# A second-stage table with zeros cleared on the chip and weight columns 128 apart, an inverse on 64-row tiles, and a new order of the operations

## The chip, the core and the metric

The kernel runs on one core of a Trainium2 chip. The metric is the device time of one execution in microseconds. The core has five engines that run side by side and meet at semaphores: TensorE (PE in the profile, its weight loads PEld), VectorE (DVE), ScalarE (ACT), GpSimd (POOL) and SyncE (SP), which here issues nearly all DMAs.

## The reference, cut to what matters

Two kinds of layers alternate, each twice, on a sequence of 2048 rows of 512 channels in bf16: a convolution layer A and a two-layer perceptron B.

```python
def _A_ref(q, k, v, shift_k, ssm_k, ssm_D):
    for t in range(ks):                       # ks = 4
        k_shift = k_shift + k_pad[:, t:t + S, :] * shift_k[:, ks - 1 - t][None, None, :]
    kv = k_shift * v
    kv_f = rfft(kv padded to 2 * S along the sequence)
    kf_f = rfft(ssm_k padded to 2 * S)
    y = irfft(kv_f * kf_f)[first S rows]
    y = y + kv * ssm_D[None, None, :]
    return q * y

def _B_ref(x, w1, b1, w2, b2):
    y = _layernorm(x, axis=-1)
    h = _gelu(jnp.einsum("bsd,df->bsf", y, w1) + b1)
    return jnp.einsum("bsf,fd->bsd", h, w2) + b2

x = A_q
x = x + _A_ref(_layernorm(x), A_k, A_v, A_shift_k, A_ssm_k, A_ssm_D)
x = x + _B_ref(_layernorm(x), B_w1, B_b1, B_w2, B_b2)
x = x + _A_ref(_layernorm(x), A_k, A_v, A_shift_k, A_ssm_k, A_ssm_D)
x = x + _B_ref(_layernorm(x), B_w1, B_b1, B_w2, B_b2)
```

The convolution of `k_shift * v` with `ssm_k` doesn't depend on `x`, so the kernel computes it once and uses it in both A layers. `ssm_D` is folded into the filter's first tap.

## The kernel before, in words

**The convolution as matmuls.** The sequence is treated as two halves of 1024 rows. Each half goes through a transform of two stages on TensorE. The first stage (`stage1`, matmuls on line 553) works on 64 groups of 8 channels and writes a real and an imaginary part to the two column halves of the array, 16 matmuls to a tile (a tile here is a piece of the accumulator memory, PSUM, that one group of matmuls fills and one or two evictions empty). The second stage (`stage2`, line 565) has 128 weight matrices of 128 x 128, one for each frequency index, in an on-chip table `R_S2` of 128 partitions x 16384 elements; a tile is 16 matmuls, each with its own weight load and 64 streamed columns. Eight tiles make one transform. It is used four times: the filter's first and second half (operations tagged `h2_0` and `h2_1`) and the signal's (`x2_0` and `x2_1`). Each weight matrix is mostly zeros: the 8 channels of a group don't mix, so an input partition (real or imaginary, position a, channel d) feeds only the 16 outputs of the same channel d. The table comes from memory with its zeros, 4 MB, in 16 DMAs (`tload` with `t_s2`). After it stand products on DVE (line 464 through `tt`), half of them with a copy of the filter whose real and imaginary partitions are exchanged by DMA (`swap`).

The inverse has two stages as well. `inverse1` (line 665) multiplies with two small tables in `R_U` (128 x 128 each), 16 matmuls of 128 streamed columns to a tile, in pairs that accumulate, and 8 tiles to a half (`i1_0`, `i1_1`). Its weights are the products, read with a distance of 4 elements between columns. `inverse2` (line 683) follows (`i2_0`, `i2_1`). `turn` (line 536) and `shift_turn` (line 585) transpose on TensorE; the weights of `turn` are read 8 elements apart, those of `shift_turn` and `stage2` contiguously. The short shift filter is `shift` (line 610, matmuls of 64 rows in two row halves of the array) and `shift_pair` (line 638, four row quarters).

**The rows.** The rows of half 0 go through both pairs of layers in blocks of 128 or 256 rows, those of half 1 in blocks of 512: statistics (tags `q`, `z`; DVE and POOL), normalising (lines 822 and 823), products and sums (`y`), a transpose, the first matrix (`m1`, line 886) with the gelu on ACT (line 891), the second matrix (`m2`, line 920) with the sum on DVE (line 924). Half 0 can start when the inverse of the first half is done; the second half's transforms run between the `m1` and `m2` matmuls of half 0.

**The order.** The builder first lists 1185 operations, each with the engines that can run it, a duration and what it reads and writes. Three hand-made tables then settle everything: `SEQ` (the order of all operations), `ENGS` (the engine of those that have a choice) and `BANKS` (the PSUM banks of each tile). Each engine gets its operations in the order of `SEQ` and runs them strictly in that order; `sync` puts in the semaphore waits. Operations 4 to 15 load the filter's, k's and v's first half; 16 to 31 are the 16 table loads. In the order before, the table loads stand on SP between the loads of the first 25 us. The eviction helper is `evac` (ACT on line 469, DVE on line 470).

Of the kernel before, what the change touches and what calls it, by code (L numbers as in the profile page):

```python
# [36 lines left out]
class Prog:  # L37
# [4 lines left out]
    G = 4  # L42
    LAT = 155.0
    SEQ = (
# [53 lines left out]
    ENGS = ("apvpvvvpavaavaaaaaavvvaaavvvpvpvaavaaaaavaavvaaaaaaaavavaaaaaavaaavaaaaaappppaaaaaaaaaaaaaaaaaaaaaaaaaaaaapvvp"  # L98
            "paappvppaappvvvpaappaappaappaappaappaappvavpaappvappaappvvppvvvpaappvvavvvvvvavpvvvvppavavpvvvvvpvaaavpvvaaapv"
            "avva")  # L100
    BANKS = ("02220326464004602026041320002442462264542202240064064646402046462667062260046446220462640604660406064226644472"
             "44450442172316353547502206314500451400554567076567013226140174645320543403764701436154766316307007062272260403"
# [243 lines left out]
def _tables():  # L346
# [9 lines left out]
    c, s = np.cos(th), np.sin(th)  # L356
# [604 lines left out]
```

## Time and profile before

| what | value |
|---|---|
| median of 3 runs | 238.67 us (238.3 to 239.51) |
| profiled execution, its span | 238.6 us |
| ScalarE, VectorE busy | 67%, 75% of the span |
| moved by DMA | 26.75 MB |
| mean granted TensorE clock | 0.993 |

The span is that of one execution under the profiler. A row of a group gives the line, the engine, the operation, the names and shapes, how often it occurs, the busy time, the mean of one in ns, and the idle time of its engine before it with what ended it. Matmuls are pipelined: the duration of one is longer than the distance to the next, so what a matmul costs in a stream is read from the start of a run of them to the start of what follows, as the chain of waits gives it. In a table by stretches each engine's busy time in us stands with its number of instructions, and the last columns are the granted clock, the DMA engines' share and the GB/s moved.

### The profile page before, as it was taken

The page shows a single profiled execution, that of the slowest core. Times are in us where ns is not written, and L with a number is a line of the kernel's source. Part 1 is how long each engine was busy: PE and PEld are TensorE (multiplying, and loading weights), DVE is VectorE, ACT ScalarE, POOL GpSimd, SP SyncE. Part 2 cuts the span into 40 slices and gives each one's busy share as a digit, 9 for nine tenths or more (in the row PEclk, how much of TensorE's full clock was granted, in tenths as well). Part 3 has the DMA queues.
Part 4 walks back from the last instruction along what each step waited for, and adds up shares of the span by engine and source line. Part 5 has one row for each costly group of instructions (what it writes and reads, how often), then busy time and mean ns, then how long its engine had stood idle before and what let it go on. Part 6 is the DMA issues. An engine that isn't in the chain of part 4 may idle for free.

```text
span 238.6 us, 6251 instructions
## 1 busy us (share of the span) xinstructions
PE 226.9 (95%) x2615; PEld 152.3 (64%) x2637; DVE 178.1 (75%) x358; ACT 159.6 (67%) x255; POOL 55.3 (23%) x120
## 2 busy tenths in 40 slices
PE   6998698899999999999999999999999999999995
PEld 3897588885968588667769675644445444444454
DVE  0579869999999999999999999593579469404013
ACT  2586879999996899999768786359036606831630
POOL 2421030104623506446004522303020210200000
PEclk9999979999999999999999999999999999999999
DMA  6999767989946660053100304200300050132202
GB/s 173 350 393 388 272 181 186 257 267 194 163 87 197 153 140 3 1 69 103 54 0 15 80 0 83 49 3 12 78 0 3 18 157 0 25 66 91 84 0 91
DMA packets 41112, 26.75 MB, mean 112 GB/s; under 512 B 23702, under 2 KB 33788, under 8 KB 41084
## 3 DMA queue, kind: packets, MB, share of 16 engines
q1 hardware_dynamic: 40786, 26.20, 40.5%
q8 instruction: 21, 0.34, 0.6%
q10 hardware_dynamic: 298, 0.16, 0.3%
q14 instruction: 7, 0.06, 0.1%
HBM read 15.07 MB, written 2.10 MB: 72 GB/s over the span
## 4 chain that ended last, share of the span: by engine, by line
PE 83%; DVE 6%; DMA 4%; ACT 3%; issue 2%; POOL 1%; SPq 1%; POOLq 0%
PE ps L886 32%; PE ps L920 31%; PE ps L665 6%; PE ps L553 5%; PE ps L565 3%; ACT ar L469 3%; DMA ar<-in_A_ssm_k_dram 2%; DVE ar L464 2%; DMA ar<-ar 2%; DVE ar L616 1%; PE ps L683 1%; PE ps L909 1%; PE ps L638 1%; PE ps L610 1%; DVE ar L470 1%
## 5 line engine op out<-in xcount | busy, mean ns | idle before, releaser
L891 ACT ACTIVATE ar<-ps,sm 128x256 bf16<-128x256 f32 (+4 forms) x143 | 65.4, 525 | 41.0 <-PE ps L886 39.5
L469 ACT ACTIVATE ar<-ps 128x1024 bf16<-128x1024 f32 (+3 forms) x77 | 71.3, 1005 | 16.4 <-PE ps L553 6.4
L886 PE MATMUL ps<-ar 128*128 128x256 bf16 (+4 forms) x568 | 81.5, 297 | 0.3
L920 PE MATMUL ps<-ar 128*128 128x512 bf16 (+1 forms) x324 | 77.2, 379 | 1.1 <-issue 0.3
L886 PEld LDWEIGHTS ps<-ar 128*128 128x128 bf16 (+1 forms) x572 | 52.8, 100 | 28.1 <-ACT ar L891 0.4
L464 DVE TENSOR_TENSOR ar<-ar 128x512 bf16<-128x512 bf16 (+3 forms) x105 | 62.7, 637 | 0.9 <-ACT ar L469 0.4
L920 PEld LDWEIGHTS ps<-ar 128*128 128x128 bf16 (+1 forms) x341 | 32.4, 98 | 33.4 <-ACT ar L891 0.2
L924 DVE TENSOR_TENSOR ar<-ar,ps 128x512 bf16<-128x512 bf16 x31 | 20.7, 678 | 33.2 <-PE ps L920 33.0
L797 DVE BATCH_NORM_STATS2 sm<-ar 128x6 f32<-128x512 bf16 x64 | 42.9, 683 | 0.5
L822 ACT ACTIVATE ar<-ar,sm 128x512 bf16<-128x512 bf16 x34 | 26.4, 811 | 9.5 <-DVE sm L809 8.3
L804 POOL TENSOR_TENSOR sm<-sm 128x2 f32<-128x2 f32 (+2 forms) x26 | 23.6, 909 | 23.8 <-DVE sm L802 22.0
L802 POOL TENSOR_SCALAR sm<-sm 128x2 f32<-128x2 f32 (+2 forms) x21 | 6.4, 304 | 97.3 <-DVE sm L798 97.1
L553 PE MATMUL ps<-ar 128*64 128x128 bf16 x512 | 18.6, 227 | 3.1 <-issue 1.4
L565 PEld LDWEIGHTS ps<-ar 128*128 128x128 bf16 x512 | 18.4, 102 | 3.4 <-ACT ar L469 1.0
L565 PE MATMUL ps<-ar 128*128 128x64 bf16 x512 | 19.6, 199 | 0.5 <-ACT ar L469 0.4
L553 PEld LDWEIGHTS ps<-ar 128*64 128x64 bf16 x512 | 15.7, 114 | 6.1 <-issue 2.6
L812 POOL TENSOR_SCALAR sm<-sm 128x1 f32<-128x1 f32 x43 | 16.1, 390 | 2.0
L470 DVE CAST ar<-ps 128x1024 bf16<-128x1024 f32 x11 | 13.3, 1222 | 4.3 <-PE ps L565 2.8
L665 PE MATMUL ps<-ar 128*128 128x128 bf16 x256 | 15.0, 219 | 0.5 <-DVE ar L464 0.4
L665 PEld LDWEIGHTS ps<-ar 128*128 128x128 bf16 x256 | 14.7, 113 | 1.2 <-DVE ar L464 0.6
L823 DVE TENSOR_SCALAR ar<-ar,sm 128x512 bf16<-128x512 bf16 x30 | 11.8, 410 | 3.4 <-POOL sm L812 3.1
L470 DVE COPY ar<-ps 128x1024 bf16<-128x1024 bf16 (+1 forms) x9 | 5.5, 632 | 8.0 <-PE ps L516 5.3
(41 smaller groups left out, 94.3 us busy)
## 6 DMA issues: line engine op xcount, KB each, us to landing
ar<-tab_s SPq DMA_DIRECT2D x16, 256.0 KB, 9.0
ar<-ar SPq DMA_DIRECT2D x16, 256.0 KB, 3.7
ar<-in_A_ssm_k_dram SPq DMA_DIRECT2D x8, 256.0 KB, 6.8
ar<-in_A_q_dram SPq DMA_DIRECT2D x8, 256.0 KB, 4.7
ar<-in_A_v_dram SPq DMA_DIRECT2D x8, 256.0 KB, 6.1
out_dram<-ar SPq DMA_DIRECT2D x7, 256.0 KB, 2.5
ar<-in_B_w_dram SPq DMA_DIRECT2D x4, 344.0 KB, 4.8
ar<-in_B_w_dram SPq DMA_DIRECT2D x5, 256.0 KB, 4.0
```

The source lines that it names most:

```text
L464: return P.op(eng, lambda e: e.tensor_tensor(o, a, b, op), dur, reads=[a, b] + list(more), writes=[o])
L469: return e.activation(dst, src(), AF.Copy)
L470: return e.tensor_copy(dst, src())
L553: r = e.matmul(Q(tl, 64 * ri, 64, i * 128, [1, 128]), w, m, start=True, stop=True)
L565: r = e.matmul(Q(tl, 0, 128, i // 8 * 512 + i % 8 * 4, [32, 16], [1, 4]), w, m, start=True, stop=True)
L665: r = e.matmul(Q(tl, 0, 128, i * 128, [1, 128]), w, m, start=n == 0, stop=n == 1)
L797: P.op(DVE, lambda e, sj=sj, x=x: e.bn_stats(sj, x), 600.0, reads=[x], writes=[sj])
L804: P.op(POOL, lambda e: e.tensor_tensor(r, v, hf, ALU.pow), 420.0 + 149.0 * n, reads=[v, hf], writes=[r])
L822: return e.activation(o, x, AF.Identity, bias=u, scale=r)
L886: r = e.matmul(Q(tl, 0, rows, 0, [1, w]), a, m, start=dk == 0, stop=dk == 3)
L891: P.op(ACT, lambda e, dst=dst, tl=tl, rows=rows, bias=bias, w=w: e.activation(dst, Q(tl, 0, rows, 0, [1, w]), AF.Gelu_apprx_tanh, bias=bia ...
L920: r = e.matmul(Q(tl, 0, 128, 0, [1, 512]), ins[fc][0], ins[fc][1], start=fc == 0, stop=fc == 10)
```

## The change

**The table.** `_tables` builds the second-stage table without its zeros: 128 rows of 2048 elements instead of 16384. On the chip it is still 128 x 16384. Eight memsets of 128 x 2048 elements (as 1024 words of 32 bits) clear it, each on DVE or POOL (six and two in the new `ENGS`); then eight DMAs of 16 partitions x 4 KB write the values, one for each channel d. The output partitions of a weight matrix are the slowest index of the table now: column m of matrix n lies at `128 * m + n`, so `stage2` reads its weights 128 elements apart. The order of the second stage's output partitions changes from (frequency, channel, part) to (channel with the even ones first, frequency, part), and `R_U` is permuted to match. The operations keep their numbers: 16 to 23 are the memsets and 24 to 31 the loads.

**The inverse.** For the second half alone, `inverse1` splits each matmul: even channels now lie in partitions 0 to 63, odd ones in 64 to 127, and `R_U` has nothing between them. A matmul of 128 rows and 128 columns becomes two of 64 rows and 64 columns, the two into different PSUM banks. The eviction reads the two banks and writes every second element.

**The order.** `SEQ`, `ENGS` and `BANKS` are new throughout. On TensorE three tiles of `h2_0` stand ahead of the first `x1_0` tile, `h2_1` and `x2_1` are spread over more of the `m1` and `m2` work, and the eight `i1_1` tiles, which stood as one and seven, stand in groups of two, two and four with `m2` work between. The evictions of `i1_1` are all on ACT, as before.

```diff
@@ Prog
-    SEQ = (33, 34, 6, 214, 1, 44, ...)
+    SEQ = (5, 18, 0, 33, 4, 2, ...)
...
@@ _tables
-    S2 = np.zeros((2, 8, 8, 128, 2, 8, 8))
-    for d in range(8):
-        S2[0, :, d, :, 0, :, d] = c
-        S2[1, :, d, :, 0, :, d] = s
-        S2[0, :, d, :, 1, :, d] = -s
-        S2[1, :, d, :, 1, :, d] = c
-    S2 = S2.transpose(0, 1, 2, 3, 5, 6, 4).reshape(128, 128 * 128)
+    S2 = np.zeros((2, 8, 8, 8, 2, 128))
+    c, s = c.transpose(0, 2, 1)[:, None], s.transpose(0, 2, 1)[:, None]
+    S2[0, :, :, :, 0] = c
+    S2[1, :, :, :, 0] = s
+    S2[0, :, :, :, 1] = -s
+    S2[1, :, :, :, 1] = c
+    S2 = S2.reshape(128, 2048)
...
-    U = U.transpose(1, 2, 0, 3, 4, 5, 6).reshape(128, 256)
+    U = U[:, :, [0, 2, 4, 6, 1, 3, 5, 7]].transpose(2, 1, 0, 3, 4, 5, 6).reshape(128, 256)
@@ the kernel
-    for i in range(16):
-        tload(t_s2, 128 * 128, i * 1024, R_S2 + i * 1024, 1024)
+    for i in range(8):
+        z = A(0, 128, R_S2 + 2048 * i, [1, 2048])
+        P.tag = "zero"
+        P.op((DVE, POOL), lambda e, z=z: e.memset(z.bitcast(U32), 0), {DVE: 1090.0, POOL: 1060.0}, writes=[z])
+        P.tag = ""
+    for d in range(8):
+        o = bass.AP(ar, d * AR + R_S2 + 2048 * (d % 2 * 4 + d // 2), [[8 * AR, 16], [1, 2048]])
+        src = bass.AP(t_s2, d * 2048, [[8 * 2048, 16], [1, 2048]])
+        P.op(SP, lambda e, o=o, src=src: e.dma_start(o.bitcast(U16), src), 475.0, writes=[o], dma=True, nbytes=1 << 16)
@@ stage2
-    ins = [(i, A(0, 128, R_S2 + (16 * t + i) * 128, [1, 128]), A(0, 128, G + (16 * t + i) * 8, [1024, 8], [1, 8])) for i in range(16)]
+    ins = [(i, A(0, 128, R_S2 + 16 * t + i, [128, 128]), A(0, 128, G + (16 * t + i) * 8, [1024, 8], [1, 8])) for i in range(16)]
@@ inverse1
-                    ins.append((i, n, A(0, 128, r + (dg // 4) * 512 + dg % 4, [4, 128]), A(0, 128, R_U + n * 128, [1, 128])))
+                    o = r + (dg // 4) * 512 + dg % 4
+                    if split:
+                        for g in range(2):
+                            ins.append((512 * g + 4 * i, n, A(64 * g, 64, o, [4, 128]), A(64 * g, 64, R_U + n * 128 + g, [8, 16], [2, 4])))
+                    else:
+                        ins.append((i * 128, n, A(0, 128, o, [4, 128]), A(0, 128, R_U + n * 128, [1, 128])))
...
+            if split:
+                evac(BOTH, A(0, 128, Z + 64 * j, [1, 2], [512, 16], [2, 32]),
+                     lambda tl=tl: Q(tl, 0, 128, 0, [512, 2], [32, 16], [1, 32]), E1, tl)
+                continue
...
-    inverse1(R_1, R_2, R_3)
+    inverse1(R_1, R_2, R_3, False)
...
-    inverse1(HH, HI, R_Z1)
+    inverse1(HH, HI, R_Z1, True)
```

More of the change, by code (lines that the diff above doesn't have):

```diff
@@ L44 @@
     SEQ = (
[53 rows of a table removed]
[L98 to L102, printed above, removed]
-             "71655156407602371631706316706615043246755274432051240747516203416017010")
[55 rows of a table added]
+    ENGS = (
+            "vpvvpvvvavvpvpvpvaaaaaaavavvavaavvavpvvvaaaaaaavvvvvaaaaavaaaaaaaavaaaaaavvaaaaaappppaaaaaaaaaaaaaaaaaaa"
+            "aaaaaaaaaappvppvapvvppaapvvvpvaappvappaappaappaappaavpaappaappaappaappvavpvavvvvpvvvaapvvavvvpaavvpvvvva"
+            "vvvvvvvpvvvapvvavvpvavva")
+    BANKS = (
+            "05277624046006264422663752422666420000144400046264606204206046406223026200046220202602626062024464262024"
+            "06641006645732463252463525277376457051675476454667075356764763455254260015462337667245654323775322347030"
+            "51166643626005341746143120240503471047132130440047272752243007067201466071432067643")
     def __init__(self, nc):
@@ L452, in dma @@
         return o
-    U16 = mybir.dt.uint16
+    U16, U32 = mybir.dt.uint16, mybir.dt.uint32
     def tload(t, row, off, dst_off, n, eng=SP):
@@ L651, in hap, with inverse1 @@
         return A(0, 128, r + 64 * t + (4096 * g if g else 0), [d, 2], [512, 16 if g is None else 8], [1, 64])
-    def inverse1(p, q, Z):
+    def inverse1(p, q, Z, split):
         for j in range(8):
@@ L660, in inverse1 @@
                 for n, r in enumerate((p, q)):
-                    ins.append((i, n, A(0, 128, r + (dg // 4) * 512 + dg % 4, [4, 128]), A(0, 128, R_U + n * 128, [1, 128])))
+                    o = r + (dg // 4) * 512 + dg % 4
[4 more added lines that the diff above has]
+                        ins.append((i * 128, n, A(0, 128, o, [4, 128]), A(0, 128, R_U + n * 128, [1, 128])))
             def f(e, ins=ins, tl=tl):
                 for i, n, w, m in ins:
-                    r = e.matmul(Q(tl, 0, 128, i * 128, [1, 128]), w, m, start=n == 0, stop=n == 1)
+                    r = e.matmul(Q(tl, 0, 128, i, *([32, 16], [1, 4]) if split else ([1, 128],)), w, m, start=n == 0, stop=n == 1)
                 return r
-            P.op(PE, f, 16 * 56.0, reads=[x for y in ins for x in y[2:]], tile=tl)
+            P.op(PE, f, 32 * 14.0 if split else 16 * 56.0, reads=[x for y in ins for x in y[2:]], tile=tl)
+            if split:
+                evac(BOTH, A(0, 128, Z + 64 * j, [1, 2], [512, 16], [2, 32]),
+                     lambda tl=tl: Q(tl, 0, 128, 0, [512, 2], [32, 16], [1, 32]), E1, tl)
+                continue
             evac(BOTH, A(0, 128, Z + 64 * j, [512, 16], [8, 8], [1, 8]),
```

108 rows, old and new, of the table SEQ are left out of this document.

## The prediction

> **What bounds the kernel now.** I read the page's head first, then the same span by stretches.
>
> ```profile
> span 238.6 us, 6251 instructions
> PE 226.9 (95%) x2615; PEld 152.3 (64%) x2637; DVE 178.1 (75%) x358; ACT 159.6 (67%) x255; POOL 55.3 (23%) x120
> ```
> ```profile
> core 0: us, PE busy (x) PEld busy (x) DVE busy (x) ACT busy (x) POOL busy (x), PEclk, DMA share, GB/s
> 0.00:8.00 8.00, 5.81 (x32) 3.27 (x33) 1.10 (x3) 2.13 (x2) 2.27 (x10) 1.00 0.70 202
> 8.00:28.00 20.00, 18.58 (x443) 16.58 (x441) 15.56 (x23) 14.92 (x17) 3.81 (x11) 1.00 1.00 371
> 28.00:44.00 16.00, 12.79 (x322) 11.70 (x319) 13.60 (x21) 13.42 (x15) 2.41 (x7) 0.89 0.75 191
> 60.00:124.00 64.00, 63.18 (x902) 47.84 (x913) 63.40 (x110) 55.95 (x112) 24.14 (x41) 1.00 0.41 90
> 124.00:133.00 9.00, 8.95 (x137) 7.98 (x137) 8.86 (x26) 7.27 (x10) 3.88 (x10) 1.00 0.15 31
> 133.00:236.00 103.00, 102.47 (x533) 52.48 (x541) 59.54 (x148) 50.48 (x87) 14.10 (x30) 1.00 0.17 43
> ```
>
> There are two regimes. From 60 us on, TensorE idles 1.4 us in 176 (0.82, 0.05 and 0.53): whatever is added to or taken from its queue there moves the end by the same amount. DVE is as full until 133 us (72.26 of 73), so taking TensorE work out before that would help less. Before 60 us no engine is full. Between 8 and 44 us TensorE idles 1.42 + 3.21 = 4.6 us, so a cost added there is paid after that much of it has been absorbed. All 32 second-stage tiles (L565) lie in these two regimes, 16 in each; the second half's inverse (L665) lies at 124.8 to 132.8 us, where TensorE is the bound.
>
> **The change part by part.** The sum is made against the profiled execution, 238.6 us; the runs' median, 238.67 us, is the same within 0.1.
>
> *Weight columns 128 apart.* A second-stage tile is 16 matmuls, each with a weight load of its own. Before, the 128 columns of a load lie side by side; now each column is 128 elements, 256 bytes, from the next. The trace has loads at three column distances: L585 and L565 at one element, L665 at 4 (8 bytes), L536 at 8 (16 bytes).
>
> ```profile
> L585 PEld LDWEIGHTS ps<-ar x32: 97/98/104, 12.8 to 14.5; 128*128 128x128 bf16 x32
> L565 PEld LDWEIGHTS ps<-ar x512: 95/98/132, 23.3 to 110.4; 128*128 128x128 bf16 x171
> L665 PEld LDWEIGHTS ps<-ar x256: 111/113/133, 43.9 to 132.5; 128*128 128x128 bf16 x128
> L536 PEld LDWEIGHTS ps<-ar x64: 143/150/172, 5.2 to 37.9; 128*128 128x128 bf16 x64
> ```
> ```profile
> 37.46 0.57 PEld L536 LDWEIGHTS ps<-ar 128*128 128x128 bf16 x8
> ```
> ```profile
> 13.03 1.79 PE ps L585 x32
> ...
> 108.79 0.47 PE ps L565 x16
> ...
> 126.49 6.26 PE ps L665 x112
> ```
>
> The middle number is a load's median duration: 98, 113 and 150 ns. What a tile pays is the cadence. Contiguous: 1.79/32 = 55.9 ns for a 128-column matmul and 0.47/16 = 29.2 ns for the second stage's 64-column one. At 8 bytes still 6.26/112 = 55.9. At 16 bytes the eight loads of one tile take 0.57 us with the last one's 0.15 in it, so (0.57 - 0.15)/7 = 60 ns, above the 55.9 that the same 128-column stream needs at L585. I read that the strided load itself lasts about 60 ns and has become the limit; behind a 64-column stream it would show in full. No row has 256 bytes. From below: if the 60 is the stream plus 4 to 6 ns, the second stage goes to 35 ns. From above: the slowest element rate nearby is DVE's, 1222 ns for 1024 elements, which would make 128 columns 153 ns.
>
> ```profile
> L470 DVE CAST ar<-ps 128x1024 bf16<-128x1024 f32 x11 | 13.3, 1222 | 4.3 <-PE ps L565 2.8 <-PE ps L553 1.4
> ```
>
> I take 61 ns, by L536, the widest distance there is. That is 61 - 29.2 = 32 ns a matmul and 16 x 32 = 0.51 us a tile. The 16 tiles of the second half (h2_1, x2_1) cost 8.2 us, all in the regime where TensorE sets the end. The 16 of the first half (h2_0, x2_0) cost 8.2 us too, less the 4.6 us of idle time: 3.6 us.
>
> [...]
>
> *Table load.* Sixteen loads of 256 KB become eight of 64 KB: 3.67 MB less, 9.9 us of a queue that moves 371 GB/s between 8 and 28 us. What waited for a DMA on TensorE there is little:
>
> ```profile
> PEld ps L516 <- DMA ar<-tab_small: 1.4, 1, 1.4
> ...
> PEld ps L536 <- DMA ar<-in_A_ssm_k_dram: 0.6, 1, 0.6
> ```
>
> Neither is the table, and the first of them is the start itself. I take -1.0 us for earlier arrivals and the new order of the early work; between 0 and -3 is possible. The clearing is six memsets on DVE and two on POOL. POOL's nearest row is 0.52 us for half the bytes:
>
> ```profile
> 0.73 0.52 POOL L501 MEMSET ar<- 128x512 bf16 x1 [0.29 <-POOLq L946]
> ...
> 6.30 0.69 DVE L470 COPY ar<-ps 128x1024 bf16<-128x1024 bf16 x1 [0.81 <-PE ps L536]
> ```
>
> DVE has no memset; by its 1024-element rows one takes 0.69 to 1.22 us, six take 4.1 to 7.3. DVE has nothing of weight to do before 6.3 us, so the idle start hides most; the excess delays the first turn's eviction by 0 to 1.3 us. I take +0.5. One wait is new: a tile's weights now span all eight blocks, so the first tile needs the whole table, and SP issues the eighth load only after a memset that stands late in POOL's order (behind the first block's statistics); loads of the second half's filter and of A_q stand behind it on SP.
>
> ```profile
> 23.29 1.03 PEld L565 LDWEIGHTS ps<-ar 128*128 128x128 bf16 x32
> ```
> ```profile
> ar<-tab_s SPq DMA_DIRECT2D x16, 256.0 KB, 9.0
> ...
> ar<-tab_small SPq DMA_DIRECT2D x1, 64.0 KB, 5.4
> ```
>
> Before, the first tile ran at 23.3 us, behind loads that took 9.0 us to land. A 64 KB load took 5.4; issued by 15 us, after the last memset, it lands ahead of 23.3, so I cost this wait at nothing. Without that cover, with the memset a few us later, the first tiles are late by the same few us.
>
> *The inverse on 64-row tiles.* Its 128 matmuls of 128 rows and 128 streamed columns become 256 of 64 rows and 64 streamed columns, two at a time on the two row halves of the array. That two row halves run together shows at L610:
>
> ```profile
> L610 PE MATMUL ps<-ar x88: 189/243/280, 15.8 to 21.0; 64*128 64x256 bf16 x40, 64*128 64x64 bf16 x16, 64*128 64x128 bf16 x16, 64*128 64x192 bf16 x16
> ```
> ```profile
> 15.83 1.89 PE ps L610 x44
> ...
> 87.61 0.57 PE ps L553 x16
> ...
> 90.90 1.46 PE ps L553 x48
> ```
>
> 44 matmuls there took 43 ns each at 186 streamed columns in the mean, half of what one by one would take (L585's 55.9 for 128 columns scales to 81). With the second stage's 29.2 ns for 64 columns, a pair takes 29.2 where one matmul took 55.9: 128 x 26.7 = 3.4 us gained. The bounds are 55.9 (loads at 8 bytes one after the other: no gain) and 29.2. Changing the tile shape costs: L553 has 16 in 0.57 and 48 in 1.46 us, so 27.8 ns each and 0.12 us for the change. In the new order the eight inverse tiles stand in three groups among m2 work, six changes at 0.11: +0.7 us. Net -2.7 us, in the regime where it counts. The evictions stay eight on ACT; m2 and m1 work stands in TensorE's queue between them and the next stage.
>
> *The new order* otherwise permutes the same operations; I cost it at nothing beyond the above, since from 60 us on there is 1.4 us to win.
>
> **Sum:** 238.6 + 8.2 + 3.6 - 1.0 + 0.5 - 2.7 = 247.2, about 247 us.
>
> **The rivals.**
>
> *Free columns.* The load's distance doesn't matter at 256 bytes, or is hidden. Then 238.6 - 1.0 + 0.5 - 2.7 = 235.4. For it: L665's loads at 8 bytes keep the cadence of 55.9. Against it: L536's 150 ns and 60 ns. The point from which it decides: a load below 29 ns. [...] Chance 0.12.
>
> *A fixed surcharge.* A strided load adds 6 ns to whatever it meets: 512 x 6 = 3.1 us, of which the first half's 1.5 vanish in idle time. 235.4 + 1.5 = 236.9. Chance 0.06.
>
> *Distance keeps growing the price*, as from 113 ns at 8 bytes to 150 at 16. With a load of 122 ns, twice L536's, a matmul costs 93 ns more: 23.8 us in the second half and 23.8 - 4.6 = 19.2 in the first. 235.4 + 43.0 = 278. The rows show two steps of growth and none beyond 16 bytes, so they can't exclude it; the nearest row stays the likelier value. Chance 0.12.
>
> *The split doesn't pair.* Loads of the two row halves follow one another: pairs stay near 56 ns and only the shape changes remain, 247.2 + 3.4 = 250.6. Against it: L610, whose loads are contiguous. Chance 0.08.
>
> **How the numbers follow.** The forecast has 0.62, and its own range, with a load of 55 to 70 ns and 0 to 6 us paid in the first half, is 243 to 253. The range of 233.5 to 256 takes in the split's failure, the fixed surcharge and the free columns, and leaves out the growing price and the tails, under 0.2. A measurement here tells about 0.5% from no change. Faster: the free columns and most of the surcharge, 0.17. Same: 0.03. Slower: 0.80.
>
> **What would show it.** L565's loads (under the changed line) at about 150 ns instead of 98, and 16 matmuls in about 1.0 us instead of 0.47; the inverse's second half in 29 ns a pair with 0.1 us at each change of shape; TensorE still full after 60 us; the first m1 work (60.40 us before) some 3 us later. Wrong it is if the second stage keeps 0.47 us a tile, or if TensorE's queue has gaps where the table is awaited.

## The result and the profile after

| | before | after |
|---|---|---|
| median of 4 runs | 238.52 us (238.3 to 239.51) | 299.87 us (298.86 to 300.37) |
| span of the profiled execution | 238.6 us | 297.8 us |
| mean granted TensorE clock | 0.993 | 0.914 |

The change makes the kernel slower by a quarter: the ratio is 1.2566, with an interval of 1.2525 to 1.2608. An execution of the changed kernel lasts 1.8 us longer than its span (299.6 and 297.8 us in the profiled one), so below spans stand against spans: 59.2 us more. That the span before, 238.6 us, lies so near the median of 238.52 us is chance: by the same 1.8 us it belongs to an execution of about 240.4 us (an estimate).

The changed kernel's page, its head and the granted clock in 40 slices of the span:

```profile
span 297.8 us, 6512 instructions
PE 281.1 (94%) x2765; PEld 200.8 (67%) x2765; DVE 222.2 (75%) x373; ACT 189.2 (64%) x252; POOL 67.2 (23%) x110
...
PEclk9995956559968999999998987999999999999999
```

TensorE has 54.2 us more of busy time. But DVE has 44.1 us and ACT 29.6 us more as well, and the clock sits at 0.5 to 0.6 for part of the first half. The second stage is now line 576 (565 before), the loads of which the view of one line gives, with minimum, median and maximum in ns:

```profile
L576 PEld LDWEIGHTS ps<-ar x512: 202/278/338, 20.3 to 166.5; 128*128 128x128 bf16 x171
```

A load has a median of 278 ns, where 98 stood before and about 150 were expected. The chain of waits gives what a tile of 16 pays (start, duration, what):

```profile
14.55 0.95 POOL ar L503
15.51 0.03 issue
15.53 4.69 DMA ar<-tab_s
20.23 0.09 issue
20.32 6.03 PE ps L576 x48
...
34.13 4.06 PE ps L576 x32
...
81.23 1.90 PE ps L576 x16
...
88.69 1.43 PE ps L906 x12
```

A tile takes 1.90 to 2.03 us (6.03/3, 4.06/2) where it took 0.47. The first `m1` work (L906) begins at 88.69 us instead of 60.40. The first four rows show the new wait: the last memset on POOL, the table's last load behind it, and the first tile.

The same span by stretches (columns as before):

```profile
8.00:28.00 20.00, 17.77 (x313) 16.53 (x314) 14.59 (x21) 10.50 (x11) 7.43 (x20) 0.87 0.69 213
28.00:44.00 16.00, 16.00 (x213) 14.81 (x211) 11.25 (x10) 11.94 (x9) 0.91 (x2) 0.74 0.21 61
44.00:60.00 16.00, 15.92 (x133) 15.80 (x133) 10.98 (x9) 10.17 (x6) 0.00 (x0) 0.58 0.70 214
133.00:236.00 103.00, 98.16 (x861) 64.46 (x860) 82.88 (x148) 71.74 (x105) 34.95 (x32) 0.95 0.16 34
```

From 44 to 60 us TensorE counts as busy almost without a gap (15.92 us) but runs 133 matmuls in 16 us, each behind its load (15.80 us of loads), at a granted clock of 0.58. Next to no idle time is left there that could absorb anything.

Divided at two marks, the first `m1` matmul and the last load of the second half's inverse (L665 at 132.5 us before, L681 at 190.9 after), the 59.2 us are 28.3 (88.7 against 60.4), 30.1 (102.2 against 72.1) and 0.8 (106.9 against 106.1). So the loss lies where the second-stage tiles lie, half in each half of the transforms.

The groups of instructions by form show that the second stage is not alone, and that the memsets are only 5.5 of DVE's 44.1 us. Of the changed kernel:

```profile
L473 ACT ACTIVATE ar<-ps 128x1024 bf16<-128x1024 f32 x68 | 85.2, 1324 | 28.5 <-PE ps L576 18.8 <-PE ps L564 6.2 <-PE ps L681 2.8
L468 DVE TENSOR_TENSOR ar<-ar 128x2048 bf16<-128x2048 bf16 x24 | 36.7, 1576 | 0.8 <-ACT ar L473 0.8
...
L503 DVE MEMSET ar<- 128x1024 uint32 x6 | 5.5, 912 | 1.8 <-PEq L966 1.0 <-issue 0.8
```

and the same two of the kernel before:

```profile
L469 ACT ACTIVATE ar<-ps 128x1024 bf16<-128x1024 f32 x67 | 64.2, 1041 | 10.3 <-PE ps L553 6.4 <-PE ps L665 2.3 <-PE ps L565 1.4
L464 DVE TENSOR_TENSOR ar<-ar 128x2048 bf16<-128x2048 bf16 x24 | 28.1, 1213 | 0.0
```

The same 24 products cost 1576 ns instead of 1213 in the mean, the evictions 1324 instead of 1041. The timeline of the changed kernel around one pair of tiles shows when:

```profile
140.32 3.19 ACT L473 ACTIVATE ar<-ps 128x1024 bf16<-128x1024 f32 x1
...
140.77 4.08 PEld L576 LDWEIGHTS ps<-ar 128*128 128x128 bf16 x32
...
141.03 4.87 DVE L468 TENSOR_TENSOR ar<-ar 128x512 bf16<-128x512 bf16 x3
141.10 5.36 POOL L824 TENSOR_TENSOR sm<-sm 128x2 f32<-128x2 f32 x1 [8.61 <-DVE sm L822]
```

While the 32 loads run (140.77 to 144.85 us), one eviction takes 3.19 us, three products 4.87 and one operation of two elements on POOL 5.36 (its line's median is 0.71; spans on POOL are rough). Sorted over the whole trace, DVE's 2048-element products have a median of 1214 ns when no second-stage load runs beside them, and the longest, of which nine tenths lie beside such loads, takes 4316; ACT's 1024-element evictions have a median of 1024 ns outside, and of 2210 for the six of which nine tenths or more lie inside. The granted clock is 1.00 from 138 to 146 us, around that pair of tiles, so this hold-up doesn't come from the clock. So there are two things that the forecast did not have: a load at twice the price, and a hold-up of the other engines.

### The profile page after: what moved, and what is told of

It is laid out like the page before. It is cut to its first block, busy times and chain, and to the rows that moved or that the text cites. A ratio compares the mean times of both kernels' runs of the same rounds, so it can differ in the third digit from the quotient of the medians.

```text
span 297.8 us, 6512 instructions
## 1 busy us (share of the span) xinstructions
PE 281.1 (94%) x2765; PEld 200.8 (67%) x2765; DVE 222.2 (75%) x373; ACT 189.2 (64%) x252; POOL 67.2 (23%) x110
## 4 chain that ended last, share of the span: by engine, by line
PE 69%; POOL 10%; DVE 8%; ACT 8%; issue 2%; DMA 2%; POOLq 0%; ACTq 0%
PE ps L906 22%; PE ps L940 20%; PE ps L576 14%; ACT ar L473 6%; PE ps L564 6%; POOL sm L832 4%; POOL sm L824 3%; DVE ar L468 3%; PE ps L703 2%; PE ps L681 2%; PE ps L547 2%; ACT ar L842 2%; DVE ar L503 2%; DMA ar<-tab_s 2%; POOL sm L822 1%
## 5 line engine op out<-in xcount | busy, mean ns | idle before, releaser
L473 ACT ACTIVATE ar<-ps 128x1024 bf16<-128x1024 f32 (+3 forms) x76 | 91.3, 1275 | 32.7 <-PE ps L576 18.8
L911 ACT ACTIVATE ar<-ps,sm 128x256 bf16<-128x256 f32 (+5 forms) x143 | 72.7, 587 | 40.8 <-PE ps L906 40.5
L906 PE MATMUL ps<-ar 128*128 128x256 bf16 (+3 forms) x572 | 85.1, 306 | 3.5 <-ACT ar L911 3.5
L468 DVE TENSOR_TENSOR ar<-ar 128x512 bf16<-128x512 bf16 (+3 forms) x105 | 81.6, 832 | 8.1 <-ACT ar L842 6.2
L906 PEld LDWEIGHTS ps<-ar 128*128 128x128 bf16 (+1 forms) x572 | 54.8, 105 | 31.4 <-ACT ar L911 4.3
L576 PE MATMUL ps<-ar 128*128 128x64 bf16 x512 | 65.6, 294 | 3.2 <-ACT ar L473 1.6
L576 PEld LDWEIGHTS ps<-ar 128*128 128x128 bf16 x512 | 64.8, 276 | 5.4 <-ACT ar L473 2.4
L832 POOL TENSOR_SCALAR sm<-sm 128x1 f32<-128x1 f32 x33 | 22.8, 707 | 1.6
L774 DVE SCALAR_TENSOR_TENSOR ar<-ar,sm,ps 128x512 bf16<-128x512 bf16 x16 | 16.8, 1186 | 2.5 <-PE ps L576 2.4
L681 PEld LDWEIGHTS ps<-ar 64*128 64x128 bf16 (+1 forms) x384 | 11.9, 113 | 2.4 <-issue 1.5
L681 PE MATMUL ps<-ar 64*128 64x64 bf16 (+1 forms) x384 | 12.5, 203 | 0.7 <-issue 0.6
```

The source lines that it names most:

```text
L468: return P.op(eng, lambda e: e.tensor_tensor(o, a, b, op), dur, reads=[a, b] + list(more), writes=[o])
L473: return e.activation(dst, src(), AF.Copy)
L576: r = e.matmul(Q(tl, 0, 128, i // 8 * 512 + i % 8 * 4, [32, 16], [1, 4]), w, m, start=True, stop=True)
L681: r = e.matmul(Q(tl, 0, 128, i, *([32, 16], [1, 4]) if split else ([1, 128],)), w, m, start=n == 0, stop=n == 1)
L832: o = e.tensor_scalar(x, y, z, -1.0, ALU.mult, ALU.mult)
L906: r = e.matmul(Q(tl, 0, rows, 0, [1, w]), a, m, start=dk == 0, stop=dk == 3)
```

## The experiments

Ratios are to the kernel before, run on the same chip beside each. From rows of a raw trace I worked out the cadence, the distance from the start of one second-stage matmul to the next inside a tile: 29.2 ns before, 122.9 ns after. The low clock doesn't make the load slow: the tiles of the changed kernel that run at full granted clock have a median of 122 ns (19 tiles), those at half of it 123 ns (13 tiles). A contiguous second-stage matmul does depend on it: in the raw trace of the kernel before it takes 29 ns at full clock and 53 ns at half (three tiles that lie wholly in the stretch at half clock).

### Columns side by side, columns apart, and time alone

The first three kernels keep the change's order, split and table values, but bring the whole table, 4 MB with its zeros, by 16 loads and without memsets. In `e1_contig` the columns of a matrix lie side by side; `e2_full128` has them 128 elements apart; `e3_repeat4` is the first with each second-stage matmul issued four times, so that TensorE is kept as long as by slow loads, without any distance.

```diff
-    for i in range(8):
+    for i in range(16):
+        tload(t_s2, 16384, i * 1024, R_S2 + i * 1024, 1024)
...
e1, e3: A(0, 128, R_S2 + (16 * t + i) * 128, [1, 128])
e2:     A(0, 128, R_S2 + (16 * t + i) // 128 * 16384 + (16 * t + i) % 128, [128, 128])
e3:     for _ in range(4):
            r = e.matmul(...)
```

> The changed kernel with the whole 4 MB table loaded as before (16 loads of 256 KB where the eight small loads stood, no memsets) and weight columns side by side; split inverse and new order as in the change. Theory (the distance of the weight columns, by what it does to TensorE and to the other engines, is the whole loss): 234 to 238 us, a second-stage tile back at 0.47 us, DVE's 2048-element products back at 1.21 us, granted clock near 0.99. Rival (the new order with its POOL and SP waits loses by itself): 245 us or more, the loss in POOL's rows of the chain.

> The same 16 loads and no memsets, but the weight columns 128 elements apart as in the change. Theory (distance alone): 297 to 303 us, loads of about 276 ns, a tile in 1.9 us. Rival (the memsets, and the wait of the first tile for the whole table, carry a part): 285 to 293 us.

> The contiguous kernel with each second-stage matmul issued four times (same result): TensorE spends 4 x 29.2 = 117 ns a matmul, as the strided loads made it, but with contiguous loads. If TensorE's time alone makes the loss: 295 to 303 us, like the change. If the strided loads also hold up DVE, ACT and POOL and let the clock drop: 270 to 283 us, DVE's products at 1.21 us, clock near 0.99.

Measured: `e1_contig` 252.19 us (ratio 1.0551, 1.0506 to 1.0596), `e3_repeat4` 286.98 us (1.2001, 1.1942 to 1.2059), `e2_full128` 303.1 us in its profiled execution, the shortest of four (the others took 309 to 312.6 us). I compare the profiled ones: 253.9, 287.7 and 303.1. `e1_contig` came out as its rival expectation had it (245 us or more), `e2_full128` at the upper end of its first, and `e3_repeat4` between its two.

The column distance alone, with nothing else changed, costs 303.1 - 253.9 = 49.2 us. So the distance, and not the memsets, the split or the order, is where most of the 61 us come from. Of `e3_repeat4` the view of the line, and of `e2_full128` the same:

```profile
L574 PEld LDWEIGHTS ps<-ar x2048: 95/98/103, 21.9 to 161.6; 128*128 128x128 bf16 x187
```
```profile
L573 PEld LDWEIGHTS ps<-ar x512: 207/277/347, 29.7 to 175.9; 128*128 128x128 bf16 x171
```

Four contiguous loads keep TensorE 4 x 29.2 = 117 ns, one at 256 bytes 123 ns (cadence in the raw trace). Yet the first costs 287.7 - 253.9 = 33.8 us and the second 49.2. The 6 ns of difference are 512 x 6 = 3 us, so about 12 us are something that the mere occupation of TensorE doesn't bring. The groups by form say what, first of `e3_repeat4`, then of `e2_full128`:

```profile
L472 DVE TENSOR_TENSOR ar<-ar 128x2048 bf16<-128x2048 bf16 x24 | 28.1, 1218 | 5.4 <-ACT ar L477 5.4
```
```profile
L472 DVE TENSOR_TENSOR ar<-ar 128x2048 bf16<-128x2048 bf16 x24 | 34.4, 1513 | 0.0
```

Beside contiguous loads DVE's products keep their 1218 ns, and the granted clock of that kernel is 1.000; beside strided ones they take 1513 ns, at a clock of 0.904. How the 12 us divide between slower engines and lower clock was not separated; `rd64` below bears on it.

`e1_contig` at 252 us, 13 us above the kernel before, is not a clean measure of the rest of the change: the sixteen loads in the new order delay others. Its chain of waits has

```profile
17.80 10.66 DMA ar<-in_B_b_dram
28.48 3.91 DMA ar<-in_B_b_dram
```

a load of a small bias that stands behind the table and keeps POOL waiting. The next kernels avoid this.

### The distance, with the change's own table and waits

These kernels are the changed one, with its memsets, its eight small loads and the same waits; only the elements that `stage2` reads as weights are others of the same table, at other distances, so the numbers computed are not the transform's. The expectations stand in the order `rd1` (2 bytes), `rd8` (16), `rd16` (32), `rd120` (240), `rd64` (128), `rd112` (224). "Conflict" in them is a name for whatever made a matmul at 256 bytes take 122.9 ns; no run shows what that is.

```diff
-A(0, 128, R_S2 + 16 * t + i, [128, 128])
+A(0, 128, R_S2 + (16 * t + i) * 128, [1, 128])      # rd1
+A(0, 128, R_S2 + (16 * t + i) * 120, [8, 128])      # rd8
+A(0, 128, R_S2 + 16 * t + i, [120, 128])            # rd120
+A(0, 128, R_S2 + (16 * t + i) * 64, [64, 128])      # rd64; rd16 and rd112 likewise
```

> The changed kernel, with its memsets, small loads, order, split inverse and waits for the whole table, but the 128 columns of each weight are read side by side from the same memory: the weights are then other numbers of the table, so the transforms' values are wrong and only the time counts. Theory (distance is the loss; the order's and the split's own worth is within 5 us of nothing): 235 to 243 us, a second-stage tile 0.47 us, DVE's 2048-element products 1.21 us. Rival (the new order loses by itself, as the 252 us of the contiguous kernel could mean): 250 us or more.

> The same, columns read 8 elements (16 bytes) apart; values wrong, time alone counts. By L536's row of before: 61 ns a matmul, loads of 147 to 150 ns, a tile about 1.0 us; DVE and ACT held up little. Rival (the price came from the 64-column stream, not from the distance): 35 ns or 120 ns.

> The same, 16 elements (32 bytes) apart; values wrong. If the price grows with the distance: between 61 and 121 ns a matmul, about 75. [...]

> [...] If the price grows with the distance: 115 to 121 ns a matmul, as at 128. [...]

> [...] Distances of 8, 16 and 120 elements gave 60 to 62 ns a matmul and 253.4 to 253.8 us, 128 gave 123 ns and 299.9. If only multiples of 256 bytes meet the conflict: 61 ns and 253 us. If it comes in at smaller powers of two: 80 to 123 ns.

> [...] If it is 256 bytes that conflict: 61 ns and 253 us.

| kernel | distance, bytes | median load, ns | cadence, ns | time, us |
|---|---|---|---|---|
| rd1 | 2 | 98 | 29.2 | 245.94 |
| rd8 | 16 | 168 | 61.3 | 253.41 |
| rd16 | 32 | 166 | 62.2 | 253.36 |
| rd64 | 128 | 220 | 90.0 | 273.20 |
| rd112 | 224 | 168 | 60.5 | 253.38 |
| rd120 | 240 | 163 | 60.3 | 253.77 |
| the change | 256 | 278 | 122.9 | 299.87 |

`rd1` was timed in rounds (ratio 1.0283, 1.0254 to 1.0313), the other five ran once each; against steps of 7 to 46 us that is enough. `rd1` and the change differ in the distance alone, with the same memsets, loads and waits: it costs 53.9 of the 61.3 us. `rd1` itself lies between its two expectations, 3 us above the first. The rows of the line in `rd8`, `rd120` and `rd64`, one after the other:

```profile
L576 PEld LDWEIGHTS ps<-ar x512: 141/168/175, 20.8 to 126.8; 128*128 128x128 bf16 x171
```
```profile
L576 PEld LDWEIGHTS ps<-ar x512: 139/163/178, 20.2 to 127.3; 128*128 128x128 bf16 x171
```
```profile
L576 PEld LDWEIGHTS ps<-ar x512: 165/220/251, 20.4 to 146.6; 128*128 128x128 bf16 x171
```

At 16, 32, 224 and 240 bytes there is one price, some 61 ns, and no growth with distance: 240 bytes cost what 16 do. Two distances fall out, 128 and 256 bytes: 90.0 ns and 122.9, twice the 61. Sixteen bytes less than 256 would have saved 46 us (253.77 against 299.87). Why these two are dearer was not shown. Neither 64 bytes nor more than 256 was tried.

The hold-up of the other engines was seen at 256 bytes alone. By the groups, first of `rd8`, then of `rd64`:

```profile
L468 DVE TENSOR_TENSOR ar<-ar 128x2048 bf16<-128x2048 bf16 x24 | 28.1, 1215 | 1.0 <-ACT ar L473 1.0
```
```profile
L468 DVE TENSOR_TENSOR ar<-ar 128x2048 bf16<-128x2048 bf16 x24 | 28.2, 1220 | 3.1 <-ACT ar L473 3.1
```

The products take 1215 ns at 16 bytes, at a granted clock of 1.000. At 128 bytes, where a load is already dearer, they still take 1220, but the granted clock is 0.943. So the dearer load and the lower clock come without the hold-up. The time from `rd8` to `rd64` grows by 19.8 us, of which TensorE's loads make 512 x (90.0 - 61.3) = 14.7. The 5 us between are not the hold-up, which doesn't show there; the lower clock would fit, but was not shown to be their cause.

### The split inverse alone

`e4_split` is the kernel before, in its own order and with its own contiguous table (the order of a matrix's 128 outputs permuted to match), with the second half's inverse on 64-row tiles as in the change. `e5_split_ev` turns the three loops of the eviction round, so that it writes neighbouring elements and does its jump between the two banks on the reading side:

```diff
-evac(BOTH, A(0, 128, Z + 64 * j, [1, 2], [512, 16], [2, 32]),
-     lambda tl=tl: Q(tl, 0, 128, 0, [512, 2], [32, 16], [1, 32]), E1, tl)
+evac(BOTH, A(0, 128, Z + 64 * j, [512, 16], [2, 32], [1, 2]),
+     lambda tl=tl: Q(tl, 0, 128, 0, [32, 16], [1, 32], [512, 2]), E1, tl)
```

> The kernel before in its old order, with the split inverse of the second half alone (contiguous table with the output partitions reordered, all 4 MB loaded). The inverse there is one and seven tiles, four changes of shape. Theory (two row halves run together, 29 ns a pair): 3.4 - 0.4 = 3.0 us less, 235.5 us. Rival (loads one after the other, or the evictions of ACT take over): 237.5 to 239.

> The old order with the split inverse, as before in the split alone (241.0 us, eight evictions of 1.22 us on ACT after one another), but the eviction reads the two banks in turn and writes side by side instead of every second element. If the scattered writes made it slower: 0.93 us an eviction, TensorE's stretch 2 us shorter, 238 to 239.5 us. If it is the reading across banks or the split itself: no change, 240.5 to 241.5.

Measured: `e4_split` 241.03 us, ratio 1.0066 (1.0035 to 1.0098): a loss where a gain of over 1% was expected. `e5_split_ev` 238.19 us, ratio 0.9958 (0.993 to 0.9986). The timelines of the inverse, first of `e4_split`, then of `e5_split_ev`, then of the kernel before:

```profile
125.00 9.80 ACT L469 ACTIVATE ar<-ps 128x1024 bf16<-128x1024 f32 x8 [0.96 <-PE ps L670]
...
129.00 0.61 PEld L670 LDWEIGHTS ps<-ar 64*128 64x128 bf16 x32 [0.50 <-ACT ar L469]
```
```profile
126.18 6.52 ACT L469 ACTIVATE ar<-ps 128x1024 bf16<-128x1024 f32 x7 [0.39 <-PE ps L670]
```
```profile
126.33 6.42 PE L665 MATMUL ps<-ar 128*128 128x128 bf16 x112
127.43 6.52 ACT L469 ACTIVATE ar<-ps 128x1024 bf16<-128x1024 f32 x7 [0.52 <-PE ps L665]
```

The matmuls did pair: a tile's 32 loads run 0.61 us with the last one's 0.11 in it, which is 0.50/31 = 16 ns each, 32 a pair, against 55.9 before. But in this kernel a tile's banks come free only with an eviction, and the rows name ACT as what TensorE waited for (0.50 us before the 32 loads of `e4_split`). In `e4_split` an eviction lasts 9.80/8 = 1.22 us; in `e5_split_ev` it lasts 6.52/7 = 0.93, as before. The edit changes the order of reading along with that of writing, but only the writing becomes less scattered by it, so I put the 0.29 us down to the writing of every second element. A tile before kept TensorE 16 x 55.9 = 0.89 us, just under ACT's 0.93. ACT was the second bound, a hair's breadth behind, and it now sets the stretch. In the stretch from 124 to 133 us, TensorE's busy time falls from 8.95 us before to 6.78 in `e4_split`:

```profile
124.00:133.00 9.00, 6.78 (x262) 5.39 (x262) 8.86 (x26) 7.97 (x8) 4.42 (x11) 0.93 0.17 32
```

`e6_inter` tries to use the freed time: it is `e5_split_ev` with the inverse's tiles in pairs and three `m2` tiles (operations 735 to 737) moved between them; their `BANKS` change too.

```diff
 SEQ:
-722, 682, 732, ..., 866, 364, ...
-683, 867, 813, 736, 374, 372, 737, 373, ...
+722, 732, ..., 866, 682, 735, 364, ..., 361, 736, 358, ..., 357, 737, 362, ...
+683, 867, 813, 374, 372, 373, ...
```

> The old order with the split inverse and the eviction that writes side by side (238.2 us), and the eight inverse tiles in four groups of two with one or two of the m2 pieces that followed them in between (their banks moved to two pairs in turn). TensorE there waited about 1.2 us for ACT's evictions of 0.93 us. If the rest of the split's gain lies in those waits: 236 to 237.5 us, TensorE busy throughout 124 to 132 us. If ACT's evictions or DVE set the end of that stretch: no change from 238.2.

Measured: 239.0 us, ratio 0.9974 (0.9952 to 0.9995), no better than `e5_split_ev`, as the second of the two expectations had it. Its timeline:

```profile
133.12 1.67 PE L692 MATMUL ps<-ar 128*128 128x512 bf16 x7 [1.51 <-ACT ar L469]
```

The moved work left TensorE waiting 1.51 us for the last evictions ahead of `inverse2`. Eight evictions of 0.93 us in a row are 7.4 us, however TensorE's queue is arranged.

### The eviction in the changed kernel

`rd1_ev` is `rd1` with the eviction of `e5_split_ev`.

> The changed kernel with contiguous weight reads (values wrong, time alone counts; 245.9 us) and, besides, the eviction that writes side by side. If the slow eviction of the inverse's second half carries a good part of the 7.3 us over the kernel before, as it did in the old order (241.0 against 238.2): 242 to 244 us. If the early order carries it (the exchange by DMA and the first inverse late, first m1 at 64.7 instead of 60.4 us): 245 to 246.

Measured: 245.07 us, ratio 1.0223 (1.018 to 1.0265), against 1.0283 for `rd1`. The intervals overlap a little; the difference of 0.6 points, 1.4 us, is half of what the same edit brought in the kernel before (1.0066 to 0.9958, 2.6 us). The time lies, just, where it was expected if the early order carries the loss. So with the columns side by side and a good eviction the change still costs some 5 us. `rd1`'s chain of waits shows where time is lost early:

```profile
39.44 4.92 DMA ar<-ar
...
44.99 1.90 DVE ar L468 x3
46.89 0.05 issue
46.94 10.21 PE ps L681 x128
```

and the same place in the kernel before:

```profile
35.67 3.98 DMA ar<-ar
...
43.91 3.76 PE ps L665 x64
47.68 0.14 issue
47.81 3.73 PE ps L665 x64
```

The exchange of the filter's partitions by DMA ends 4.7 us later (44.36 against 39.65), so the first inverse starts 3.0 us later. It then takes 10.21 us instead of 7.63, in a stretch (44 to 60 us) whose granted clock is 0.79: in the raw trace 56 of the 127 distances between its matmuls are 107 ns, the others 56. `rd1`'s first `m1` load stands at 64.7 us, 4.3 after the kernel before. What the memsets alone cost in this was not tried.

## Why the prediction was wrong

The direction was right and the size was not: 247 us forecast, 299.87 measured, above the upper end of 256.

**The price of a column at 256 bytes is the step that failed.** The prediction said: "I take 61 ns, by L536, the widest distance there is." For what L536 shows this was exact: `rd8` has its distance of 16 bytes and a cadence of 61.3 ns. It holds at 240 bytes too. At 256 bytes it is 122.9 ns. The upper bound named there, 153 ns from a DVE row, was the side on which the answer lay: 512 x (153 - 29.2) less 4.6 us of idle time is 58.8, and 235.4 + 58.8 = 294 us. That this comes near 299.87 is luck, since a load costs 123 ns and not 153, and the rest of the time is lost elsewhere. But the bound was worked out and then dropped from the range.

**What a load of 61 ns would have cost** was forecast as 11.8 us, of which 3.6 in the first half. From `rd1` to `rd8` it is 7.5 us, but the two don't compare cleanly. The first inverse starts 2.4 us later in `rd8` than the 46.94 us of `rd1`, so the first half does pay:

```profile
49.34 4.78 PE ps L681 x80
```

Its matmuls then take 4.78/80 = 60 ns each at full clock, where those of `rd1` took 10.21/128 = 80, and it is done in 7.45 us (raw trace) instead of 10.21. So the first `m1` load moves only from 64.7 to 64.9 us. With these 2.8 us added back the loads cost some 10 us, an estimate, not far below the 11.8.

**Two readings of the kernel before** were wrong, with little weight. The forecast adds the change to a span, 238.6 us, and takes its nearness to the median execution for agreement, though an execution lasts some 1.8 us longer than its span. And the 32 second-stage tiles don't lie 16 and 16 in the two stretches named: in the raw trace four of the second half run from 56.4 to 58.4 us, ahead of the stretch that TensorE fills (TensorE idles 1.06 us between 44 and 60 us).

**The hold-up of other engines had no term.** The sum treated the second stage as TensorE's own affair. Of the 49.2 us by which `e2_full128` exceeds `e1_contig`, some 12 are not explained by TensorE's time. The lower granted clock, 0.914 on the mean and 0.58 from 44 to 60 us, had no term either.

**The rivals.** "Distance keeps growing the price" had the load right, 122 ns, for a reason that the sweep refutes: 240 bytes cost no more than 16. With 278 us it was still 22 short: 10.5 us because the kernel without the distance takes 245.94 us and not 235.4, the other 11 because the distance cost 53.9 us and not 43.0. "Free columns" and the "fixed surcharge" fell: at every distance tried from 16 bytes on, a second-stage matmul took 60.3 ns or more against 29.2. "The split doesn't pair" fell too, since pairs take 32 ns, though its result, no gain, came true by another way.

**The inverse** was sized at -2.7 us and gave +0.7% in `e4_split`. The gain on TensorE was there (55.9 to 32 ns a pair); the step that failed is "The evictions stay eight on ACT", which costed them as unchanged. They were 1.22 us instead of 0.93, and even at 0.93 they stood right behind the matmuls that were sped up, so the best case is -0.4%.

**The table load, the memsets and the new wait.** A memset on DVE takes 0.91 us, inside the forecast 0.69 to 1.22. The wait for the whole table exists (TensorE idles 1.6 us on it in the changed kernel, a gap of the kind that the prediction named as a sign against it) and ends at 20.3 us, earlier than the first tile before (23.3). No run took it away alone.

**The new order** was costed at nothing, with -1.0 us for earlier arrivals. With the columns side by side the change stands at +7.3 us (245.94 against 238.65), where these terms and the split made -3.2. About 1.4 us of the 10.5 us between is the eviction's writing order; the late exchange and the slow first inverse are seen in the trace. In the old order the split inverse missed its term by 4.3 us (+1.6 in `e4_split` instead of -2.7), the eviction's part included; whether that carries over to the new order, and the rest, was not taken apart.

## What to carry to other kernels

Before a weight is read with a distance between its columns, measure that very distance: here 256 bytes cost 122.9 ns a matmul, twice the 60.3 of 240, and 128 half as much again (90.0), so columns 16 bytes closer avoided it (a longer distance was not tried). When a price is unknown and the bounds are far apart, the range has to keep both. Look for a slow access in the other engines' durations too, since the same DVE product at 1.2 us in one place and 4.3 in another points to something outside of DVE. When a matmul is made faster, compare the next engine's time for the same tile first: here 0.89 us on TensorE stood against 0.93 on ACT, so half the matmul time was worth 0.4%, and `e5_split_ev` at 238.19 us (0.9958, 0.993 to 0.9986) is the best version found, just ahead of the kernel before.

## What the runs showed of the hardware that was not expected

- A matmul of 64 streamed columns with a weight load of 128 columns: 29.2 ns with the columns side by side (`rd1`), 60.3 to 62.2 ns at 16, 32, 224 and 240 bytes (`rd8`, `rd16`, `rd112`, `rd120`), 90.0 ns at 128 (`rd64`) and 122.9 ns at 256 (the changed kernel).
- Beside loads at 256 bytes, in the changed kernel, instructions of DVE and ACT took longer: a DVE product went from 1214 to as much as 4316 ns, an ACT eviction from 1024 to 2210 (medians, the second of six), and, by rough spans, a POOL operation from 0.71 to 5.36 us. At 128 bytes (`rd64`) the DVE product kept 1220 ns in the mean.
- From 44 to 60 us the granted clock was 0.58 in the changed kernel, whose second-stage loads fill 14.34 of these 16 us, and 0.50 in `rd64`; `e3_repeat4`, with contiguous loads there, has 1.00. The loads alone don't decide it: from 138 to 146 us the changed kernel has 1.00 with 6.12 us of such loads, and `rd1`, without a distance, has 0.79 from 44 to 60. Why it fell was not settled. In the stretches at half clock a load at 256 bytes keeps its 123 ns, and in `rd1` a matmul of 128 streamed columns goes from 56 to 107 ns.
- An ACT eviction of 1024 elements that writes every second bf16 element takes 1.22 us (`e4_split`), one that writes neighbours and jumps between banks on the reading side 0.93 (`e5_split_ev`).
